# Two tokens per partition, heads in two halves, and a new opening order in a retention and MLP kernel

## The chip, the cores and the metric

The kernel runs on one core of one Trainium2 chip. The metric is the device time of one execution in microseconds; the time before is the median of three runs. A core has TensorE (PE, with its weight loads shown as PEld), VectorE (DVE), ScalarE (ACT), GpSimd (POOL) and SyncE (SP), and 16 DMA engines that serve queues of SP, ACT and POOL.

## What is computed

The first part is a retention layer over 8 batches, 8 heads, 576 tokens and a head size of 64. The second is an MLP whose hidden activation is h cos(h).

```python
scores = scale * np.matmul(q, k.transpose(0, 1, 3, 2))        # 8 x 8 x 576 x 576, scale = 1/8
gamma = 1.0 - 2.0 ** (-5.0 - np.arange(H))
Dmat = np.where(rel >= 0, gamma[:, None, None] ** rel, 0.0)   # rel = query position - key position
attn = np.matmul(scores * Dmat, v)
x = attn.transpose(0, 2, 1, 3).reshape(4608, 512)
h = x @ w_in                                                  # 512 -> 2048
out = (h * np.cos(h)) @ w_out                                 # 2048 -> 512
```

## The kernel before

**Retention.** A batch b has five chunks r: four of 128 tokens and one of 64 (`ck_of`). Since gamma^(i-j) splits into gamma^i and gamma^-j, q is multiplied by a table UQ and v by a table WV, and the causal mask MK then only cuts. For one chunk:

- `load` (L238) brings q, k and v to fp32 staging tiles `kn`, `qn`, `vn`, with one token per partition: 8 heads of 64 numbers, so runs of 256 bytes. One DMA on SP's queue for each tensor.
- `kcast` and `decay` make bf16 tiles `kq` and `vb`. For the first two batches `cast_pe` places them on named engines; later they run on POOL.
- k and q are transposed into `kqt`: for the first two batches by TensorE with an identity (`turn`, and an ACT copy out), from batch 2 on by a DMA transpose (`prep_dma`).
- `scores` (L326) multiplies k and q for each head, 64 rows of the array for each head of a pair, into the PSUM banks `sc`; DVE masks the result into `rt` (L341).
- `rest` adds up the output in PSUM bank `po`: the state of earlier chunks times q (po<-kqt,sb) plus the masked scores times v (po<-rt,vb), then the state's own update in bank `st` (st<-vb,kq), which accumulates in PSUM over the chunks of a batch. ACT copies `po` to the bf16 activations `xt` (L386) and the state to `sb` (L390).

A *visit* (b, r) is `rest(b, r-1)` followed by `scores(b, r)`.

**MLP.** Tokens go in nine blocks j of 512. `mlp1` computes one of 16 groups dt of 128 hidden units: four matmuls into a bank, the cosine on ACT (L413), the product on DVE (L416) into `gt` (block 0: `ss`). Block 0 then runs `mlp2`, 16 parts of four plain matmuls. The blocks from 1 on run `layer2`, a scheme of seven products of half size in place of eight: 14 half steps n of eight matmuls (L487), with sums of quarters made by DVE (`ssum` for activations, `tsum` once for weights; both L467), snapshots on ACT (L490) and totals on DVE (L495). The first product reads `gt` of dt 0 to 7, the second that of dt 8 to 15.

**Order.** Everything is written out by hand in `emit`; each engine runs its instructions in the order of that list, and `Sched` adds the semaphore waits. ORDER interleaves dt 0, 8, 1, 9, ... up to 7, 15. In block j, `mlp1` is followed by `layer2` with visits of batch j+1 at n = 0, 3, 6, 9 and 12 (VISITS). Batches 0 and 1 are spread by hand over the start and over block 0's `mlp2`. `idle` issues matmuls on zeros that keep TensorE active while it has no other work.

Of the kernel before, what the change touches and what calls it, by code (L numbers as in the profile page):

```python
# [12 lines left out]
DFF = 2048  # L13
# [8 lines left out]
GR = 64  # L22
NWI = 4
# [4 lines left out]
ORDER = [8 * h + i for i in range(8) for h in range(2)]  # L28
# [10 lines left out]
def ck_of(r):  # L39
    return min(CH, S_ - CH * r)  # L40

# [16 lines left out]
class Sched:  # L58
# [54 lines left out]
    def dma(self, eng, name, fn, reads=(), writes=(), after=()):  # L113
# [6 lines left out]
        d[1] += 16  # L120
        fn(self.eng[eng]).then_inc(d[0], 16)
# [12 lines left out]
class _Kernel:  # L134
    def __init__(self, nc, es, q, k, v, w_in, w_out, out):
# [10 lines left out]

        self.KQT = [sb(f"kqt{i}", [128, 2 * NP * S_], BF16) for i in range(2)]
# [3 lines left out]
        self.KQ = [[sb(f"kq{i}_{r}", [128, 2 * DM], BF16) for r in range(NCH)] for i in range(2)]  # L151
        self.bKB = [[Buf() for _ in range(NCH)] for _ in range(2)]
        self.bQB = [[Buf() for _ in range(NCH)] for _ in range(2)]
        self.VB = [[sb(f"vb{i}_{r}", [128, DM], BF16) for r in range(NCH)] for i in range(2)]
        self.bVB = [[Buf() for _ in range(NCH)] for _ in range(2)]
        self.ST32 = {x: [sb(f"{x}n{r}", [128, DM], F32) for r in range(NCH)] for x in "kqv"}
# [10 lines left out]
        self.bSB = [Buf() for _ in range(2)]  # L167
        self.GT = sb("gt", [128, 16 * TB], BF16)
# [14 lines left out]
        self.IP = sb("ip", [128, NCH], F32)  # L183
        self.WV = sb("wv", [128, NCH * H_], F32)
        self.UQ = sb("uq", [128, NCH * H_], F32)
        self.MK = sb("mk", [128, CH], BF16)
# [12 lines left out]
        self.PO, self.bPO = ps("po"), Buf()  # L199
        self.ST, self.bST = ps("st"), Buf()  # L200
# [11 lines left out]
    def consts(self):  # L212
        s = self.s
        s.op("dve", lambda e: e.memset(self.IDLE.ap(), 0.0), writes=[self.bIDLE])
        s.op("pool", lambda e: e.iota(self.IP.ap(), [[CH, NCH]], base=0, channel_multiplier=1,
                                      allow_small_or_imprecise_dtypes=True), writes=[self.bIP])
        for t, b, fill, first, cmp in ((self.ID, self.bID, 1.0, 0.0, ALU.not_equal),
                                       (self.MK, self.bMK, 0.0, 1.0, ALU.is_ge)):
            s.op("dve", lambda e: e.memset(t.ap(), first), writes=[b])
            s.op("pool", lambda e: e.affine_select(t.ap(), t.ap(), pattern=[[1, CH]],  # L220
                                                   compare_op=cmp, fill=fill, base=0,
                                                   channel_multiplier=-1), reads=[b], writes=[b])
        s.op("dve", lambda e: e.memset(self.C_LN8.ap(), float(math.log(1.0 / 8.0))), writes=[Buf()])
        s.op("dve", lambda e: e.memset(self.C_PIH.ap(), float(math.pi / 2.0)), writes=[self.bC])
        for i in range(2):
            s.op("dve", lambda e: e.memset(self.SB[i].ap(), 0.0), writes=[self.bSB[i]])
        for t, b, sign in ((self.UQ, self.bUQ, 1.0), (self.WV, self.bWV, -1.0)):
            for h in range(H_):
                s.op("act", lambda e: e.activation(  # L229
                    bass.AP(t, h, [[NCH * H_, 128], [H_, NCH]]), self.IP.ap(), AF.Exp,  # L230
                    scale=sign * self.lng[h], **(dict(bias=self.C_LN8.ap()) if sign > 0 else {})),
                    reads=[self.bIP, self.bC], writes=[Buf()])
            b.w = [Tok("act", "act", s.count["act"], {})]
        s.op("act", lambda e: e.activation(self.JUNK.ap(), self.C_PIH.ap(), AF.Sin), reads=[self.bC])  # L234
# [3 lines left out]
    def load(self, x, b, r, after=()):  # L238
        ck = ck_of(r)
        t, bt = self.ST32[x][r], self.bST32[x][r]  # L240
        dst = bass.AP(t, 0, [[DM, ck], [D_, H_], [1, D_]])
        src = bass.AP(self.src[x], (b * H_ * S_ + CH * r) * D_, [[D_, ck], [S_ * D_, H_], [1, D_]])
        return self.s.dma("sp", f"{x}n{r}", lambda e: e.dma_start(dst, src), writes=[bt], after=after)
# [16 lines left out]

    def kcast(self, eng, b, r):
        ck, i = ck_of(r), b % 2
        o, x = bass.AP(self.KQ[i][r], 0, [[2 * DM, ck], [1, DM]]), bass.AP(self.ST32["k"][r], 0, [[DM, ck], [1, DM]])
# [3 lines left out]
    def decay(self, eng, x, b, r):  # L267
        ck, i = ck_of(r), b % 2
        t, off, pitch, bt, w, bw = ((self.KQ[i][r], DM, 2 * DM, self.bQB[i][r], self.UQ, self.bUQ) if x == "q"
                                    else (self.VB[i][r], 0, DM, self.bVB[i][r], self.WV, self.bWV))  # L270
        self.s.op(eng, lambda e: e.tensor_tensor(  # L271
            bass.AP(t, off, [[pitch, ck], [D_, H_], [1, D_]]),
            bass.AP(self.ST32[x][r], 0, [[DM, ck], [D_, H_], [1, D_]]),
            bass.AP(w, r * H_, [[NCH * H_, ck], [1, H_], [0, D_]]), ALU.mult),
            reads=[self.bST32[x][r], bw], writes=[bt])

    def kqt(self, i, c, r, n=1):
        return bass.AP(self.KQT[i], c * S_ + CH * r, [[2 * NP * S_, 128], [S_, n], [1, ck_of(r)]])

    def prep_dma(self, b, r):  # L280

        s, ck, i = self.s, ck_of(r), b % 2
# [4 lines left out]
            self.kqt(i, 0, r, 2 * NP), bass.AP(self.KQ[i][r], 0, [[2 * DM, ck], [1, 2 * DM]])),  # L287
# [3 lines left out]
    def turn(self, b, r, x, eng, sc=None):  # L291

        s, ck, i = self.s, ck_of(r), b % 2
        off, c0, bs, bd = (0, 0, self.bKB[i][r], self.bKT[i][r]) if x == "k" else (DM, NP, self.bQB[i][r], self.bQT[i][r])
# [416 lines left out]
```

## Time and profile before

| | |
|---|---|
| median of 3 runs | 314.26 us (314.18 to 314.48) |
| the profiled execution | 313.65 us, of it span 311.9 us |
| mean granted TensorE clock | 0.991 |
| PE busy | 295.5 us, 95% of the span |
| DVE, ACT, POOL busy | 226.3, 179.4, 114.5 us |
| q1, the loads and DMA transposes on SP | 141,696 packets, 36.45 MB, 66.4% of the 16 DMA engines' span |
| first `mlp2` matmul | 37.85 us |
| first product of `layer2(1)` | 80.42 us |
| from there on | blocks of about 31.2 us, two of 27.4 and 16.9 us at the end |

The span runs from the first instruction to the last; the rest of the profiled execution's time lies around it. Busy time of TensorE includes the latency of each matmul, so a busy share near one does not say that the array streams all the time; for that the starts of the single matmuls are read.

### The profile page before, as it was taken

The numbers are of one execution on the slowest core, as the hardware profiler recorded it, in microseconds if no ns is written. First come the engines' busy times: TensorE is split into PE (matmuls) and PEld (weight loads), VectorE is DVE, ScalarE is ACT, GpSimd is POOL, SyncE is SP. The second block draws the span as 40 slices with busy tenths as digits, with TensorE's granted clock in tenths as the row PEclk, the third lists the DMA queues.
The fourth block names the chain that finished last, engine by engine and source line by source line (L and its number), as shares of the span: only waits on it lengthen the run. The fifth ranks groups of instructions, "written<-read, shape, count | busy, mean of one in ns | idle before, by whom it ended". The sixth has DMA issues, their size and how long they took to land.

```text
span 311.9 us, 6946 instructions
## 1 busy us (share of the span) xinstructions
PE 295.5 (95%) x2706; PEld 189.6 (61%) x2706; DVE 226.3 (73%) x372; ACT 179.4 (58%) x333; POOL 114.5 (37%) x129
## 2 busy tenths in 40 slices
PE   7679998999899999999999999999999999999994
PEld 2345445544786468646864786478647864784483
DVE  3455824789976998599659985996599659728942
ACT  7477726577455755476547654765475547427620
POOL 2364184868474655456636555430000000000000
PEclk9999997999999999999999999999999999999998
DMA  9999999999999999999999999960110011003003
GB/s 172 226 210 199 215 207 215 214 284 197 213 193 242 255 207 187 218 253 228 180 219 265 188 196 249 239 120 2 67 69 0 2 69 68 3 18 117 2 0 135
DMA packets 150560, 49.47 MB, mean 159 GB/s; under 512 B 141824, under 2 KB 145920, under 8 KB 150528
## 3 DMA queue, kind: packets, MB, share of 16 engines
q1 hardware_dynamic: 141696, 36.45, 66.4%
q0 software_dynamic: 4224, 4.19, 8.2%
q10 hardware_dynamic: 4608, 8.39, 7.7%
q8 instruction: 21, 0.34, 0.5%
q14 instruction: 11, 0.09, 0.1%
HBM read 36.70 MB, written 9.44 MB: 148 GB/s over the span
## 4 chain that ended last, share of the span: by engine, by line
PE 84%; ACT 7%; DVE 5%; issue 2%; ACTq 0%; POOL 0%; DVEq 0%; POOLq 0%
PE mm L316 59%; PE mm L318 14%; PE po L316 6%; PE sc L316 4%; DVE gt L416 3%; ACT cb L413 2%; DVE rt L341 2%; ACT kqt L302 2%; PE st L316 1%; ACT xt L386 1%; ACT sb L390 1%; ACT uq L229 1%; DVE osb L495 0%; ACT L234 0%; ACT L229 0%
## 5 line engine op out<-in xcount | busy, mean ns | idle before, releaser
L413 ACT ACTIVATE cb<-mm,c_pih 128x512 bf16<-128x512 f32 (+2 forms) x152 | 100.5, 665 | 42.5 <-PE mm L318 39.9
L316 PE MATMUL mm<-xt,win 128*128 128x512 bf16 (+2 forms) x456 | 117.3, 368 | 0.9 <-DVE gt L416 0.5
L416 DVE TENSOR_TENSOR gt<-mm,cb 128x512 bf16<-128x512 f32 x128 | 85.6, 686 | 9.1 <-ACT cb L413 7.6
L316 PEld LDWEIGHTS mm<-xt,win 128*128 128x128 bf16 x456 | 43.3, 98 | 49.8 <-ACT cb L413 1.8
L341 DVE TENSOR_TENSOR rt<-sc,mk 128x512 bf16<-128x512 f32 (+1 forms) x80 | 47.1, 629 | 32.7 <-PE sc L318 32.4
L318 PE MATMUL mm<-xt,win 128*128 128x512 bf16 (+2 forms) x152 | 55.9, 368 | 0.0
L271 POOL TENSOR_TENSOR kq<-qn,uq 128x512 bf16<-128x512 f32 (+1 forms) x39 | 42.7, 1094 | 29.1 <-DMA qn<-in_q_dram 28.1
L490 ACT ACTIVATE sn<-mm 128x512 f32<-128x512 f32 x32 | 19.1, 597 | 43.5 <-PE mm L318 43.5
L271 POOL TENSOR_TENSOR vb<-vn,wv 128x512 bf16<-128x512 f32 (+1 forms) x36 | 39.8, 1106 | 10.7 <-DMA vn<-in_v_dram 10.3
L316 PE MATMUL mm<-tt,ss 128*128 128x256 bf16 x336 | 43.3, 273 | 0.0
L264 POOL CAST kq<-kn 128x512 bf16<-128x512 f32 (+1 forms) x39 | 26.2, 671 | 46.7 <-DMA kn<-in_k_dram 40.3
L495 DVE TENSOR_TENSOR osb<-mm,sn 128x512 f32<-128x512 f32 x32 | 22.1, 689 | 29.0 <-PE mm L318 28.8
L386 ACT ACTIVATE xt<-po 128x512 bf16<-128x512 f32 (+1 forms) x41 | 22.2, 544 | 29.9 <-PE po L318 29.5
L316 PEld LDWEIGHTS mm<-tt,ss 128*128 128x128 bf16 x336 | 31.4, 98 | 4.9
L467 DVE TENSOR_TENSOR ss<-gt 128x512 bf16<-128x512 bf16 (+1 forms) x56 | 31.4, 560 | 0.9
L316 PE MATMUL mm<-wout,gt 128*128 128x256 bf16 x224 | 28.8, 273 | 2.3 <-DVE gt L416 2.2
L316 PE MATMUL mm<-wout,ss 128*128 128x256 bf16 (+1 forms) x160 | 27.9, 309 | 0.0
L318 PEld LDWEIGHTS mm<-xt,win 128*128 128x128 bf16 x152 | 14.9, 98 | 16.6
L316 PEld LDWEIGHTS mm<-wout,gt 128*128 128x128 bf16 x224 | 20.8, 98 | 6.8 <-DVE gt L416 2.3
L390 ACT ACTIVATE sb<-st 64x256 bf16<-64x256 f32 x64 | 23.8, 372 | 0.8
L316 PE MATMUL sc<-kqt 64*128 64x128 bf16 (+1 forms) x280 | 15.3, 217 | 4.1 <-ACT kqt L302 4.1
L316 PEld LDWEIGHTS mm<-wout,ss 128*128 128x128 bf16 x160 | 15.2, 98 | 5.8 <-issue 0.7
(66 smaller groups left out, 290.7 us busy)
## 6 DMA issues: line engine op xcount, KB each, us to landing
kn<-in_k_dram SPq DMA_DIRECT2D x32, 256.0 KB, 4.7
qn<-in_q_dram SPq DMA_DIRECT2D x32, 256.0 KB, 5.1
vn<-in_v_dram SPq DMA_DIRECT2D x32, 256.0 KB, 5.5
out_dram<-osb ACTq DMA_DIRECT2D x32, 256.0 KB, 3.7
win<-in_moe_w_in_dram POOLq DMA_DIRECT2D x4, 512.0 KB, 8.2
wout<-in_moe_w_out_dram POOLq DMA_DIRECT2D x4, 512.0 KB, 10.4
kn<-in_k_dram SPq DMA_DIRECT2D x8, 128.0 KB, 4.6
qn<-in_q_dram SPq DMA_DIRECT2D x8, 128.0 KB, 4.3
```

The costliest lines, as they stand in the source:

```text
L264: fn = (lambda e: e.activation(o, x, AF.Copy)) if eng == "act" else (lambda e: e.tensor_copy(o, x))
L271: self.s.op(eng, lambda e: e.tensor_tensor(bass.AP(t, off, [[pitch, ck], [D_, H_], [1, D_]]), bass.AP(self.ST32[x][r], 0, [[DM, ck], [D_, ...
L316: self.nc.tensor.matmul(o, a, b, **kw)
L318: return s.done("pe", self.nc.tensor.matmul(o, a, b, **kw), reads, writes)
L341: s.op("dve", lambda e: e.tensor_tensor(bass.AP(self.RT[r % 2][hp], 0, p3), bass.AP(self.SC[hp], 0, p3), bass.AP(self.MK, 0, [[CH, ck], [0 ...
L386: s.op("act", lambda e: e.activation(o, p, AF.Copy), reads=[self.bPO], writes=self.bXT[x0 // GR:(x0 + n) // GR])
L390: s.op("act", lambda e: e.activation(bass.AP(self.SB[r % 2], 64 * hp * 512 + 64 * hp, [[512, 64], [128, NP], [1, D_]]), bass.AP(self.ST, 6 ...
L413: s.op("act", lambda e: e.activation(ci, mi, AF.Sin, bias=self.C_PIH.ap(), scale=1.0), reads=[bm, self.bC], writes=[bcb])
L416: s.op("dve", lambda e: e.tensor_tensor(bass.AP(gt, dt * TB + o0, [[16 * TB, 128], [1, n]]), mi, ci, ALU.mult), reads=[bm, bcb], writes=bg)
L467: self.s.op(eng, lambda e: e.tensor_tensor(oo, xx, yy, op), reads=xb + yb, writes=ob)
L490: self.s.op("act", lambda e: e.activation(self.SN[k].ap(), bank[0].ap(), AF.Copy), reads=[bank[1]], writes=[self.bSN[k]])
L495: self.s.op("dve", lambda e: e.tensor_tensor(bass.AP(self.OSB, 2 * t * DM + 256 * h, [[4 * DM, 128], [DM, 2], [1, 256]]), bass.AP(bank[0], ...
```

## The change

- **Layout.** A partition now holds two neighbouring tokens of a 128-token chunk (`ns_of` = 2; 1 in the 64-token chunk) for four of the heads: partitions 0 to 63 hold heads 0 to 3, partitions 64 to 127 heads 4 to 7. A load has runs of 512 bytes (256 in the small chunk) and is issued as two DMAs, one for each half of the partitions.
- **Retention in quarters.** `scores`, the second part of `rest` and the state update use 64x64 tiles of the array: 16 matmuls for a full chunk where 8 were. The mask becomes 128 x 256 and is made from an iota.
- **State.** Output and state update share one PSUM tensor `ps` of two banks. The state is summed in an fp32 SBUF tile `s32`: an ACT copy for r = 0, a DVE add for r = 1 to 3. `state`, split from `rest`, makes the bf16 `sb` from it.
- **ORDER** ends with 6, 7, 14, 15.
- **Beginning.** The constants come in another order, ACT loads the Exp table by a `touch` at once and the Sin table after the first state; `mlp1` can put several dt of a few tokens in one bank (k, step), and pieces of block 0's `mlp1` stand between the first chunks; weight loads, casts, idles and the steps in block 0's `mlp2` are reordered; six of the `tsum` go to POOL; block 1 starts with 448 tokens of four dt; block 0's stores are issued during block 1.

```diff
+NIP = S_ // 64
-ORDER = [8 * h + i for i in range(8) for h in range(2)]
+ORDER = [8 * h + i for i in range(6) for h in range(2)] + [6, 7, 14, 15]
...
+        def half(hs):
+            dst = bass.AP(t, 64 * hs * 256 * ns, [[256 * ns, 64], [D_ * ns, 4], [1, D_ * ns]])
+            src = bass.AP(self.src[x], ((b * H_ + 4 * hs) * S_ + CH * r) * D_,
+                          [[D_ * ns, 64], [S_ * D_, 4], [1, D_ * ns]])
+            return lambda e: e.dma_start(dst, src)
+        return self.s.dma("sp", f"{x}n{r}", [half(0), half(1)], writes=[bt], after=after)
...
     def scores(self, b, r):
+        for c in range(2):
+            for sl in range(ns):
+                for hs in range(2):
+                    for hp in range(2):
+                        k0 = 64 * hp * W + 1024 * r + c * 128 + 64 * hs
+                        mms.append((
+                            bass.AP(self.SC[hp], 64 * hs * 512 + (c * ns + sl) * nq, [[512, 64], [1, nq]]),
+                            bass.AP(self.KQT[i], k0 + sl * 256, [[W, 64], [1, 64]]),
+                            bass.AP(self.KQT[i], k0 + 256 * ns, [[W, 64], [256, ns], [1, 64]]),
...
-    def rest(self, b, r):
+    def rest(self, b, r, state=True):
...
+                o = bass.AP(self.XT, x0, [[NP * XR, 128], [XR, NP], [1, ns], [ns, n // ns]])
+                p = bass.AP(self.PS, po0, [[1024, 128], [256, NP], [64, ns], [1, n // ns]])
                 s.op("act", lambda e: e.activation(o, p, AF.Copy),
+                     reads=[self.bPS], writes=self.bXT[x0 // GR:(x0 + n) // GR])
+        if state:
+            self.state(b, r)
+
+    def state(self, b, r):
         if r < NCH - 1:
+            st = bass.AP(self.PS, 128, [[1024, 128], [256, NP], [1, D_]])
+            s32 = bass.AP(self.S32, 0, [[4 * D_, 128], [D_, NP], [1, D_]])
+            if r == 0:
+                s.op("act", lambda e: e.activation(s32, st, AF.Copy), reads=[self.bPS], writes=[self.bS32])
+            else:
+                s.op("dve", lambda e: e.tensor_tensor(s32, st, s32, ALU.add),
+                     reads=[self.bS32], writes=[self.bPS, self.bS32])
             for hp in range(2):
                 s.op("act", lambda e: e.activation(
                     bass.AP(self.SB[r % 2], 64 * hp * 512 + 64 * hp, [[512, 64], [128, NP], [1, D_]]),
+                    bass.AP(self.S32, 64 * hp * 4 * D_, [[4 * D_, 64], [D_, NP], [1, D_]]), AF.Copy),
...
     def emit(self):
...
+        self.idle(12)
+        self.cast_pe(0, 0, "pool", "dve", "dve")
         self.w_in_load(0, after=[land[0][2]])
+        self.turn(0, 0, "k", "act")
+        self.idle(3)
+        self.turn(0, 0, "q", "act")
+        self.idle(6)
         self.scores(0, 0)
...
+        self.rest(0, 0, False)
+        self.idle(1)
         self.scores(0, 1)
+        self.state(0, 0)
+        self.touch(AF.Sin)
+        self.idle(6)
...
+        self.turn(0, 2, "k", "act")
+        self.decay("dve", "q", 0, 2)
+        self.rest(0, 1, False)
+        self.turn(0, 2, "q", "act")
+        self.state(0, 1)
         self.idle(2)
         self.scores(0, 2)
...
+        for dt in (0, 2):
+            self.mlp1(0, dt, 0, 256, 2)
+        self.rest(0, 2, False)
+        self.turn(0, 3, "q", "act")
+        self.state(0, 2)
         self.scores(0, 3)
+        self.mlp1(0, 0, 256, 128, 4)
...
         steps = {0: [(turn, 0, 4)], 2: [(self.scores, 0, 4)], 4: [(self.rest, 0, 4), (turn, 1, 0)],
                  6: [(self.scores, 1, 0)],
+                 7: [(turn, 1, 1), (self.rest, 1, 0, False), (self.scores, 1, 1), (self.state, 1, 0),
+                     (self.tsum, 0, 0, 4), (self.tsum, 0, 4, 4),
+                     (self.tsum, 1, 0, 4, "pool"), (self.tsum, 2, 0, 4, "pool"), (self.kcast, "pool", 1, 3),
...
+                     (self.rest, 1, 1, False), (turn, 1, 2)],
+                 8: [(self.state, 1, 1), (self.decay, "dve", "v", 1, 2)], 9: [(self.scores, 1, 2)],
+                 11: [(self.decay, "dve", "q", 1, 3), (self.rest, 1, 2, False)],
+                 12: [(turn, 1, 3), (self.state, 1, 2)], 13: [(self.decay, "dve", "v", 1, 3)],
+                 14: [(self.scores, 1, 3)]}
...
+        part1 = TB - 64
+        for n, dt in enumerate(ORDER[:4]):
+            self.mlp1(1, dt, 0, part1)
+            if n == 1:
+                self.rest(1, 3, False)
+        for dt in (0, 1):
+            self.mlp1(1, dt, part1, 64, 2, 8)
```

More of the change, by code (lines that the diff above doesn't have):

```diff
@@ L119, in dma @@
         d = self.dsem[name]
-        d[1] += 16
-        fn(self.eng[eng]).then_inc(d[0], 16)
+        for f in fn if isinstance(fn, list) else [fn]:
+            d[1] += 16
+            f(self.eng[eng]).then_inc(d[0], 16)
         clock = {s: v for s, (v, _) in self.seen[eng].items() if s != eng}
@@ L597, in emit @@
+        self.w_in_load(1, after=[land[2][1]])
+        self.turn(0, 2, "k", "act")
[3 more added lines that the diff above has]
+        self.state(0, 1)
         self.idle(2)
         self.scores(0, 2)
[L599 to L603 removed]
+        self.decay("dve", "v", 0, 2)
+        self.kcast("pool", 0, 3)
@@ L604, in emit @@
+        self.w_in_load(2, after=[land[3][1]])
         self.w_in_load(3)
+        self.decay("pool", "q", 0, 3)
+        self.w_out_load(0)
         self.turn(0, 3, "k", "act")
-        self.rest(0, 2)
+        for dt in (0, 2):
+            self.mlp1(0, dt, 0, 256, 2)
+        self.rest(0, 2, False)
         self.turn(0, 3, "q", "act")
-        self.idle(2)
+        self.state(0, 2)
         self.scores(0, 3)
-        for dt in range(4):
-            self.mlp1(0, dt, 256, 128)
+        self.mlp1(0, 0, 256, 128, 4)
@@ L612, in emit @@
+        self.decay("dve", "v", 0, 3)
+        for dt in (4, 6):
+            self.mlp1(0, dt, 0, 256, 2)
+        self.mlp1(0, 4, 256, 128, 4)
         self.rest(0, 3)
-        self.idle(4)
-        self.w_out_load(0)
+        for dt in (8, 9):
+            self.mlp1(0, dt, 0, 384)
+        self.w_out_load(1)
         self.cast_pe(0, 4, "pool", "pool", "pool")
         self.loads_to(10)
-        self.w_out_load(1)
         self.cast_pe(1, 0, "pool", "pool", "pool")
+        self.w_out_load(2)
+        self.w_out_load(3)
```

277 lines of the change are left out of this document (134 added, 143 removed).

## The prediction

> **What bounds the kernel now.** I read the page first, then busy time by stage, the waits of TensorE, and last the order of TensorE's instructions inside one retention visit.
>
> ```profile
> PE 295.5 (95%) x2706; PEld 189.6 (61%) x2706; DVE 226.3 (73%) x372; ACT 179.4 (58%) x333; POOL 114.5 (37%) x129
> PE   7679998999899999999999999999999999999994
> ```
>
> TensorE is busy 95% of the span, so time comes off only where it starts sooner, does less, or stops waiting. The slices show where it is loose: the first ten. By stage (columns: PE, PEld, DVE, ACT, POOL busy, then clock, DMA share, GB/s):
>
> ```profile
> 0.00:27.50 27.50, 20.08 (x219) 11.32 (x220) 12.24 (x30) 18.84 (x51) 13.44 (x23) 1.00 1.19 202
> 37.85:62.53 24.68, 23.27 (x234) 12.65 (x232) 12.87 (x18) 12.13 (x26) 16.98 (x19) 0.93 1.17 213
> 62.53:80.42 17.89, 16.66 (x109) 7.40 (x105) 16.82 (x26) 13.21 (x23) 11.46 (x12) 1.00 1.15 238
> 143.25:174.45 31.20, 31.09 (x312) 21.03 (x306) 24.46 (x42) 18.59 (x34) 17.40 (x19) 1.00 1.20 223
> ```
>
> A steady block (last row) has 0.1 us of idle TensorE in 31.2. The first 80.42 us, up to the first product of `layer2(1)`, is the loose part; 11 us of its busy time is `idle` matmuls, and a stretch near 50 us ran at clock 0.5. What TensorE waits for before 80.42 us (first two lines) and after it (last line):
>
> ```profile
> PE sc L316 <- ACT kqt L302: 4.1, 5, 1.2
> PE po L316 <- DVE rt L341: 1.4, 3, 0.6
> PE mm L316 <- DVE gt L416: 2.4, 5, 0.8
> ```
>
> Early it waits on the chain transpose, ACT copy, scores, DVE mask. Later it waits only where `mlp1` ends and product 0 needs the last `gt`. No DMA is in the list. Inside a visit:
>
> ```profile
> 83.13 0.41 PE L316 MATMUL po<-rt,vb 128*64 128x128 bf16 x7
> 83.38 0.29 PE L316 MATMUL st<-vb,kq 128*64 128x64 bf16 x7
> 83.60 0.39 PE L316 MATMUL sc<-kqt 64*128 64x128 bf16 x7
> 83.93 0.94 PE L316 MATMUL mm<-wout,gt 128*128 128x256 bf16 x7
> ```
>
> Eight matmuls of po take 0.25 us, st 0.22, sc 0.33. The single records explain it: the two of a pair start 3 ns apart, pairs follow at 54 ns (128 columns) or 28 ns (64). Streaming is thus 0.22, 0.12 and 0.22 us; the rest is a gap of 95 to 102 ns at each change of array shape (128x128 to 128x64, that to 64x128, that to 128x128). From po to st, both 128x64, there is none.
>
> **Retention in quarters.** A full chunk now issues 16 matmuls of 64x64 each for scores, po and st, instead of 8. If four run at once, streaming stays at 4 x 54, 4 x 54 and 4 x 28 ns. No four-way overlap is in the trace. Cost from below: none, as the pairs of 128*64 (two streams from one partition) and of 64*128 (two PSUM banks written in one partition) each already use what a quarter needs. From above: two at a time, 8 x 54 + 8 x 54 + 8 x 28, or 0.55 us more a chunk. I take none, because both kinds of pairs, and both kinds of 64*64 pairs in the half chunk, start 3 ns apart. All three groups have one shape, so the gap between st (or po) and sc goes: 0.10 us x 29 visits after 80.42 us = 2.9. The 64-token chunk has 2 quads for 4 pairs in scores and po: 2 x 0.056 x 6 batches = 0.7.
>
> **ORDER.** Product 0 reads dt 0 to 7. Dt 7 was second to last of `mlp1`, with one group (0.86 us) behind it against 0.2 + 0.70 + 0.69 us of latency, ACT and DVE. Now two groups (1.73 us) lie behind. Gaps beyond the 0.10 of the shape change, at the transitions at 112, 143, 174, 205, 236, 267 and 294 us: 0.35, 0.18, 0.09, 0.09, 0.09, 0.42, 0.88 = 2.1 us off. Product B, which needs dt 15, comes 1.75 us later: covered.
>
> **State in SBUF.** For r = 1 to 3 a DVE add (128x256 with PSUM: 0.42 us by the 128x256 row of L416) precedes the two ACT casts, and it also waits for the ACT copy out of the shared `ps`. Queued behind it on DVE are the two masks that the next `rest` needs. Mask end to next po leaves 1.23 us at most visits, but 0.10, 0.33 and 0.19 at n = 6 of the blocks at 90, 122 and 184 us, where DVE is late with `ssum`. The add starts the masks some 0.35 later: stalls of 0.3 + 0.1 + 0.25 = 0.65 us. The casts end some 0.4 us before they are needed. The strided `xt` write is not in the trace; between 0 and twice its 0.60 us, I take 0: it lies under three products. Steady sum: -2.9 - 0.7 - 2.1 + 0.65 = **-5.0 us** (-5.7 without stalls; -3 with eight of 0.35).
>
> **Loads.** Packets of q1 cost 0.664 x 16 x 311.9 / 141696 = 23 ns for 257 bytes, q10's 83 ns for 1.8 KB; so 512 bytes cost 23 to 47 ns, nearer the low end. Early landings are 1.2 us apart per 256 KB (218 GB/s), so DMA sets that pace, not SP. SP now issues six half loads a chunk; its shortest issues take 0.38 to 0.45 us, 2.3 to 2.7 us a chunk against 3.6 between chunks now. If every issue took 0.6 us the gain would be nil, without loss. Later, nothing waits on it. POOL's 64-token ops halve (1.1 to about 0.6 us), off the path.
>
> **The beginning**, walked with rows of the trace (transposes 0.22 us, ACT copy 0.60, two copies 1.09, masks 1.29, 0.25 from the last matmul to its reader):
> - The first tile lands at 3.9 us as now. Twelve idles (cold clock, 0.43 each) end at 6.3; turn k, its ACT copy to 7.3; three idles; turn q 7.2, copy to 8.2; six idles end at 8.7: scores(0,0) at 8.8 (8.48 now). No gain yet.
> - Masks to 10.5; rest(0,0) to 10.9; an idle; scores(0,1) at 11.3 (12.66), since turn(0,1) no longer waits for a rest.
> - ACT is then one chain: xt 11.1 to 11.7, s32 12.05, two sb 12.8, the Sin table (1.28 and 0.2) 14.25, copy of k(0,2) 14.85, xt(0,1) 15.4, copy of q(0,2) 15.9: scores(0,2) at 16.0 (17.66).
> - `mlp1` of dt 0 to 3 on 256 tokens (2 x 0.87) 16.6 to 18.3. DVE: masks to 17.8, v(0,2) to 18.4. rest(0,2) 18.5 to 19.15; ACT: xt to 19.95, copy of q(0,3) 20.45: scores(0,3) at 20.5 (22.77).
> - Four more `mlp1` pieces of 0.87, to 24.3, over the masks and v(0,3); rest(0,3) to 25.05; dt 8 and 9 on 384 tokens (1.3), the 128-token rests (2.2), to 28.6. Six full dt remain, 5.2, where at 27.5 now twelve do: `mlp2` starts at **33.8 against 37.85**.
> - `mlp2` stretch: 16 x 0.863 = 13.8, transposes 2.0, five scores 1.9, four rests 2.4, together 20.1. At n = 7 scores(1,1) waits for ACT and rest(1,1) for the masks just issued: 0.3 + 0.5 + 1.6 us of waits, 0.2 of it found back. End 33.8 + 22.3 = 56.1 (62.53).
> - `mlp1(1)`: 13.8; two rests, a turn, two scores 1.9; first product at **71.8 against 80.42**, -8.6.
> - Held back: the waits at n = 7 leave TensorE nearly idle for 3.4 us, as at 47 us now, where 3.4 us at half clock followed (1.7 us lost): half of that, 0.8. Six `tsum` move to POOL, 1024 elements each, by its 512-element TENSOR_TENSOR rows about 2.1 us, up to 2.9 beside DVE; POOL ends at 62 to 66 us and `prep_dma(2, 0)` queues behind them; needed at 71. With weights: 0.6. Beginning: **-7.2 us** (0 if rival 1 takes all; -9.8 if neither happens and half the waits at n = 7 are found back).
>
> Sum on the profiled execution, 313.65 us (span 311.9 and 1.8 around it): 313.65 - 7.2 - 5.0 = 301.5. The median lies 0.6 above that execution: **302.1 us**.
>
> **Rivals.**
> 1. The beginning does not pay: ACT's copies, POOL's `tsum` or w_in and w_out landing late refill what the order empties. For it: waits there are latencies of a chain, and a chain is not shortened by order. Against: the `mlp1` pieces are real work in these waits. Saving 0 to 4: 305 to 309. Chance 0.18.
> 2. Quarters overlap, but start no faster than 14 ns each on average, the densest the trace shows (st). N = 128 hides it; st costs 16 x 14 instead of 4 x 28 ns, 0.11 x 32 chunks, and the half chunks gain nothing: +4.2, 306.3. Chance 0.08.
> 3. Slower: quarters run two at a time, 0.55 us x 32 chunks + 0.11 x 8 = 18.5 us more: 320. It decides from 12.2 / 32 = 0.38 us a chunk. Against it stand the 3 ns starts. Chance 0.11.
> 4. Slower: each matmul has a start floor of its own whatever the tile. With the 28 ns between st's pairs, sixteen take 0.45 us: +0.23 + 0.23 + 0.34 a chunk, 0.34 a half chunk, x 32 and x 8: +28, 330. Against: st's eight stream in 0.12 us, where the floor would ask 0.22. Chance 0.03. [...]
>
> **Numbers.** The forecast has 0.57; rivals 1 and 2 (0.26) are faster too. Range 298.5 (steady -5.7, beginning -9.8) to 309.5 (rival 1's end): 0.83 inside. A measurement here tells 0.2% (0.6 us) from no change: faster 0.83, same 0.02, slower 0.15 (rivals 3 and 4, and 0.01 for others).
>
> **What would show it.** Quads of sc starts within 12 ns and 54 ns apart, with st to sc at no gap, or else 108 ns a quad (rival 3). The wait on DVE gt after 80 us under 0.5 us. First `mlp2` matmul near 34 us, first product of `layer2(1)` near 72; a POOL wait or clock 0.5 between is rival 1. A mask wait of some tenths at n = 6. I am wrong if blocks last over 31 us.

## The result and the profile after

The changed kernel took 312.61 us in the median, the kernel before 315.0 us in the same set of runs: ratio 0.990, 95% interval 0.9872 to 0.9929. A second set gave 0.9937 (0.9904 to 0.997). It is faster, by 2 to 3 us, not by the 12 forecast. The profiled execution of the first set ran at a mean granted TensorE clock of 0.750, with a span of 377.8 us, and one other execution of that set took 1036.24 us; no run here explains either. So the profile shown here is that of the second set: 310.0 us at 0.998, against 311.9 us at 0.991 before.

The page after, the engines' line and TensorE's slices:

```profile
PE 288.2 (93%) x3496; PEld 188.8 (61%) x3520; DVE 234.3 (76%) x392; ACT 189.9 (61%) x336; POOL 116.6 (38%) x133
PE   8579997997999998999999999998999999999994
```

TensorE is busy for 7.3 us less, but the span is only 1.9 us shorter: most of the saved work came back as idle time. By stage (the start, `mlp2` of block 0, `mlp1` of block 1 up to the first product of `layer2(1)`, one later block):

```profile
0.00:27.50 27.50, 20.06 (x288) 12.42 (x292) 14.15 (x30) 18.17 (x43) 11.44 (x22) 1.00 0.93 192
37.82:60.62 22.80, 20.52 (x286) 10.96 (x289) 13.78 (x19) 12.28 (x26) 17.05 (x16) 1.00 1.05 213
60.62:79.52 18.90, 16.48 (x155) 8.07 (x155) 14.64 (x26) 13.88 (x26) 18.90 (x18) 1.00 0.76 203
142.50:173.58 31.08, 30.51 (x399) 20.44 (x400) 26.53 (x45) 20.34 (x36) 13.36 (x15) 1.00 0.90 191
```

`mlp2` starts at 37.82 us, as before (37.85), and the first product comes at 79.52 (80.42). The later block has 0.57 us of idle TensorE where before it had 0.1. What TensorE waits for (us in total, times, longest), the three largest before 80 us and, below the dots, all after it:

```profile
PE mm L360 <- POOL kq L306: 3.4, 3, 2.6
PE sc L360 <- ACT kqt L346: 1.9, 4, 0.7
PE ps L360 <- ACT sb L454: 1.4, 1, 1.4
...
PE ps L360 <- DVE rt L387: 2.4, 4, 1.0
PE ps L360 <- ACT sb L454: 0.9, 1, 0.9
PE sc L360 <- DMA kqt<-kq: 0.6, 2, 0.3
```

The last waits on `gt` after 80 us are gone. In their place stand waits on the mask (`rt`), on `sb` and on a DMA transpose, 3.9 us together; before, none of these was there after 80 us. Ahead of 80 us, at the end of block 1's `mlp1`, 1.3 us of waits on `gt` are left. Inside a visit:

```profile
82.33 0.33 PE L360 MATMUL ps<-rt,vb 64*64 64x128 bf16 x11
82.50 0.29 PE L360 MATMUL ps<-vb,kq 64*64 64x64 bf16 x15
82.62 0.39 PE L360 MATMUL sc<-kqt 64*64 64x128 bf16 x15
82.95 0.94 PE L360 MATMUL mm<-wout,gt 128*128 128x256 bf16 x7
```

The state update takes 0.12 us from its first matmul to the first of the scores, which follow without a gap. The single records show four matmuls 3 to 4 ns apart (82.618, 82.622, 82.625, 82.628), then the next four at 82.678. The one gap left is that to the 128x128 products, 0.10 us.

### The profile page after: what moved, and what is told of

Its sections match the earlier page's. It is cut to its first block, busy times and chain, and to the rows that moved or that the text cites. A ratio compares the mean times of both kernels' runs of the same rounds, so it can differ in the third digit from the quotient of the medians.

```text
span 377.8 us, 8676 instructions
## 1 busy us (share of the span) xinstructions
PE 363.8 (96%) x3496; PEld 216.1 (57%) x3520; DVE 234.6 (62%) x392; ACT 190.1 (50%) x336; POOL 114.0 (30%) x133
## 4 chain that ended last, share of the span: by engine, by line
PE 92%; SPq 2%; DMA 2%; ACT 1%; issue 1%; DVE 0%; POOL 0%
PE mm L360 66%; PE mm L362 16%; PE ps L360 7%; PE sc L360 3%; SPq L279 2%; DMA kn<-in_k_dram 2%; ACT kqt L346 0%; DVE osb L562 0%; ACT xt L437 0%; PE sc L362 0%; ACT sb L454 0%; ACT cb L480 0%; POOL kq L306 0%; PE ps L362 0%; ACT s L449 0%
## 5 line engine op out<-in xcount | busy, mean ns | idle before, releaser
L360 PE MATMUL mm<-xt,win 128*128 128x512 bf16 (+4 forms) x500 | 144.6, 417 | 1.0 <-ACT cb L480 0.2
L480 ACT ACTIVATE cb<-mm,c_pih 128x512 bf16<-128x512 f32 (+3 forms) x147 | 99.0, 679 | 71.9 <-PE mm L362 70.7
L483 DVE TENSOR_TENSOR gt<-mm,cb 128x512 bf16<-128x512 f32 (+1 forms) x130 | 88.3, 682 | 41.3 <-ACT cb L480 39.4
L360 PEld LDWEIGHTS mm<-xt,win 128*128 128x128 bf16 x517 | 54.1, 112 | 66.4 <-issue 60.5
L362 PE MATMUL mm<-xt,win 128*128 128x512 bf16 (+5 forms) x147 | 65.6, 446 | 0.8
L387 DVE TENSOR_TENSOR rt<-sc,mk 128x512 bf16<-128x512 f32 (+1 forms) x80 | 44.8, 602 | 18.8 <-PE sc L362 18.7
L360 PE MATMUL mm<-tt,ss 128*128 128x256 bf16 x336 | 54.4, 312 | 0.0
L437 ACT ACTIVATE xt<-ps 128x512 bf16<-128x512 f32 (+1 forms) x41 | 26.9, 660 | 39.0 <-PE ps L362 28.3
L360 PE MATMUL mm<-wout,gt 128*128 128x256 bf16 x224 | 36.0, 318 | 0.0
L454 ACT ACTIVATE sb<-s 64x256 bf16<-64x256 f32 x64 | 26.5, 415 | 12.9 <-DVE s L451 11.7
L451 DVE TENSOR_TENSOR s<-ps,s 128x256 f32<-128x256 f32 x24 | 10.2, 424 | 32.5 <-ACT xt L437 32.4
L362 PEld LDWEIGHTS mm<-xt,win 128*128 128x128 bf16 x147 | 16.5, 112 | 23.1 <-issue 22.2
```

The costliest lines, as they stand in the source:

```text
L360: self.nc.tensor.matmul(o, a, b, **kw)
L362: return s.done("pe", self.nc.tensor.matmul(o, a, b, **kw), reads, writes)
L387: s.op("dve", lambda e: e.tensor_tensor(bass.AP(self.RT[r % 2][hp], 0, p3), bass.AP(self.SC[hp], 0, p3), bass.AP(self.MK, 0, [[2 * CH, 128 ...
L437: s.op("act", lambda e: e.activation(o, p, AF.Copy), reads=[self.bPS], writes=self.bXT[x0 // GR:(x0 + n) // GR])
L454: s.op("act", lambda e: e.activation(bass.AP(self.SB[r % 2], 64 * hp * 512 + 64 * hp, [[512, 64], [128, NP], [1, D_]]), bass.AP(self.S32, ...
L480: s.op("act", lambda e: e.activation(ci, mi, AF.Sin, bias=self.C_PIH.ap(), scale=1.0), reads=[bm, self.bC], writes=[bcb])
```

## The experiments

All numbers of one kernel's stages come from its one profiled execution. A stretch of TensorE at clock 0.5 begins in most of them between 12 and 54 us (before: at 50.3 us, 3.4 us long), in the kernel before also at the very end (309.7 to 311.9 us), and in four kernels (masks_first, block1_act_b, v_on_pool, both_b, with mean clocks of 0.989, 0.978, 0.972 and 0.984) also between 77 and 95 us. By the half clock alone 3.4 us of it cost up to 1.7 us. Compare times by the ratio and stages by the table, with two bounds on both. The whole change and order_only were each measured in two sets, and their ratios differ there by 0.4%. And the two executions of order_only, one kernel, differ by 2.5 us in the first stage of the table and by 1.6 us in the last, the later one with 3.4 us of half clock at 18.7 us.

| kernel | ratio to before (95%) | `mlp2` starts | first product of `layer2(1)` | from there to the end |
|---|---|---|---|---|
| before | | 37.85 | 80.42 | 231.5 |
| after_again | 0.9937 (0.9904 to 0.997) | 37.82 | 79.52 | 230.4 |
| order_only | 0.9864 (0.9821 to 0.9908) | 37.93 | 79.09 | 231.3 |
| order_only_again | 0.990 (0.9854 to 0.9947) | 40.45 | 81.22 | 229.7 |
| after_old_order | 0.997 (0.9936 to 1.0005) | 39.03 | 82.75 | 228.8 |
| new_layout_old_begin | 1.0051 (1.0015 to 1.0087) | 44.91 | 85.26 | 227.8 |
| no_pool_from_b3 | 0.9879 (0.9831 to 0.9927) | 39.31 | 82.42 | 226.6 |
| masks_first | 1.0118 (1.0071 to 1.0166) | 39.39 | 84.22 | 236.5 |
| w_in_later | 1.002 (0.999 to 1.0051) | 40.95 | 84.06 | 226.9 |
| tsum_on_dve | 0.9958 (0.9926 to 0.9991) | 38.47 | 80.68 | 228.5 |
| two_queues | 0.993 (0.990 to 0.9959) | 37.85 | 79.69 | 228.7 |
| two_queues_w | 0.9988 (0.9955 to 1.0022) | 40.44 | 83.55 | 229.8 |
| block1_act | 0.9985 (0.9952 to 1.0017) | 39.99 | 82.20 | 226.5 |
| block1_act_b | 0.9953 (0.9908 to 0.9997) | 40.30 | 81.83 | 230.7 |
| v_on_pool | 1.0185 (1.0128 to 1.0242) | 40.38 | 88.23 | 229.3 |
| both_b | 1.0156 (1.0079 to 1.0232) | 40.01 | 85.64 | 228.9 |

### The parts: ORDER, and the beginning

**after_again** is the whole change once more, beside the parts.

> The changed kernel itself, once more, for a trace at full clock. Theory S (the steady blocks save the forecast 5 us, the new beginning gives nothing or loses 1 to 2 us): first product of layer2(1) at 80 to 83 us, blocks of about 30.4 us. Theory B (the beginning saves some 7 us, the steady blocks lose what they were to save): first product at 72 to 76 us, blocks of 31.5 us or more. Both: some 3 us below the kernel before in time.

Neither theory holds alone. The first product of `layer2(1)`, at 79.52 us, is close to theory S, but the five blocks from there last 31.1 to 32.3 us where S has 30.4: the beginning gained 0.9 us and the rest 1.0.

**order_only** is the kernel before with one line changed:

```diff
-ORDER = [8 * h + i for i in range(8) for h in range(2)]
+ORDER = [8 * h + i for i in range(6) for h in range(2)] + [6, 7, 14, 15]
```

> The kernel before with the new ORDER alone (6, 7, 14, 15 last). By the forecast 2.1 us less than before: the waits on DVE gt at the ends of mlp1 after 80 us go from 2.4 us to under 0.5. If the product sums on DVE are late anyway, the wait moves to a later half step and the time stays within 0.6 us.

It gave 0.9864, twice the gain expected, and 0.990 in another set, where it stood for comparison:

> The kernel before with the new ORDER alone, once more, for comparison on the same chip: a ratio near 0.986, about 2 us under the whole change.

The whole change beside it gave 0.9937: with overlapping intervals, but the one line alone is at least as fast as all of it. **after_old_order** is the same question from the other side, the whole change with the old line put back.

> The changed kernel with the old ORDER. By the forecast 2 us slower than the changed kernel, as the waits on DVE gt return at each end of mlp1; if ORDER does nothing, within 0.6 us of it.

It gave 0.997, and its waits from 60 us on show what the old line brings:

```profile
PE mm L360 <- DVE gt L483: 4.3, 10, 0.9
```

The wait on `gt` is 4.3 us in ten places, at the end of `mlp1` of every block; with the new line 1.3 us were left, all in block 1. In the time that is only 0.3%, or 1 us, with overlapping intervals. Other waits stand against it: those on `rt` are 0.3 us in this execution and 2.4 in that of the changed kernel.

**new_layout_old_begin** keeps layout, quarters, state and ORDER of the change, and takes the emission up to block 1 from the kernel before (idles, casts, whole `rest` with its state at once, `mlp1` pieces of one dt, `tsum` on DVE, block 0's stores at once).

```diff
         self.idle(12)
-        self.cast_pe(0, 0, "pool", "dve", "dve")
...
+        self.cast_pe(0, 0, "act", "dve", "dve")
...
+        for dt in range(4):
+            self.mlp1(0, dt, 0, 256)
...
+        self.rest(0, 2)
...
-        for dt in (0, 2):
-            self.mlp1(0, dt, 0, 256, 2)
-        self.rest(0, 2, False)
```

> The changed kernel (512-byte loads, quarters, state in SBUF, new ORDER) with the emission order of before up to block 1. Theory S: as fast as the changed kernel or faster by 1 to 2 us, some 5 us below before. Theory B: near before or above it, so 3 us or more slower than the changed kernel.

1.0051, slower than before. With the old order `mlp2` starts at 44.91 us, 7 us later than before. A stretch at half clock from 14 to 24 us explains up to 5 of them by the clock alone, and perhaps more: in order_only, 3.4 us of it went with a start 2.5 us later. So the new order of the beginning does pay, by about 1.1% or 3.6 us of time. Whether it pays by shorter waits or by keeping TensorE at its clock is not separated here. It pays back what the rest of the change loses under the old order.

### The beginning: what the loads do

Two stretches of the start tell where the loss begins (DMA share and GB/s stand last; the kernel before first, the changed one second):

```profile
0.00:9.00 9.00, 6.62 (x34) 2.62 (x35) 2.51 (x10) 6.77 (x22) 2.67 (x10) 1.00 0.98 178
```

```profile
0.00:9.00 9.00, 7.36 (x45) 3.08 (x45) 3.71 (x13) 5.36 (x20) 3.13 (x11) 1.00 0.50 145
```

In the first 9 us the DMA engines were full before and are half empty now. The timeline of SP's issues at the same place, before and after, says why:

```profile
5.98 1.14 SPq L243 DMA_DIRECT2D kn<-in_k_dram  x1
7.17 1.15 SPq L243 DMA_DIRECT2D qn<-in_q_dram  x1
```

```profile
4.80 1.28 SPq L279 DMA_DIRECT2D kn<-in_k_dram  x2
6.12 1.28 SPq L279 DMA_DIRECT2D qn<-in_q_dram  x2
```

Before, SP's issues grew from 0.45 us for the first to 1.15 us for the sixth, with the DMA engines at 0.98. Now each half takes 0.617 us (the median of all half loads of the span; in the first 9 us 0.60 to 0.62 from the second on) although the DMA engines are busy for only 0.50 of the time: with the gap between them, two make 1.28 us. The packets did become cheaper for their size. Of queue q1 in the first 40 us (packets, MB, share of 16 engines), before and after:

```profile
q1 hardware_dynamic: 19345, 4.87, 70.5%
```

```profile
q1 hardware_dynamic: 10899, 4.86, 54.0%
```

That is 0.705 x 16 x 40 us / 19345 = 23 ns for packets of 252 bytes on average, and 32 ns now for 446, but in the first 9 us nothing fills the room that this leaves. Before, k of chunk 2 landed at 11.03 us; now it lands at 15.65, with w_in's first part in flight ahead of it.

**w_in_later** holds w_in back:

```diff
-        self.w_in_load(0, after=[land[0][2]])
...
         self.cast_pe(0, 1, "pool", "pool", "dve")
+        self.w_in_load(0, after=[land[2][0]])
```

> The changed kernel with the first weight load issued on POOL after the casts of chunk 1 and after k of chunk 2 has landed (about 11.5 us) instead of after v of chunk 0 (7.3 us). Theory L (v of chunk 1 and k of chunk 2 land at 14.6 and 15.7 us because w_in's 512 KB take the DMA engines, and SP with 0.62 us an issue is too slow to have them through before): they land at 11 to 12 us, turn(0, 2, k) comes 3 to 4 us earlier, the first product of layer2(1) 2 to 3 us earlier, the time falls by 1 to 3 us. Rival (the chain on ACT sets the start): scores(0, 2) stays at 18 us or more and the time within 1 us.

k of chunk 2 landed at 12.35 us, 3.3 us earlier, but k of chunk 3 at 19.78, and TensorE waited 2.9 us for its cast. Ratio 1.002: no gain.

**two_queues** takes three half loads off SP's queue:

```diff
+        if b == 0 and r == 1:
+            t0 = self.s.dma("sp", f"{x}n{r}", [half(0)], writes=[bt], after=after)
+            self.late.append((x, half(1), bt, t0))
+            return t0
...
+            t1 = self.s.dma("pool", f"{x}b", f, writes=[Buf()])
```

> The whole change, but the second halves of the loads of chunk 1 of batch 0 (k, q, v) are issued on POOL's queue at the start, so that SP issues three DMAs fewer before chunk 2. Theory (SP's issue, 0.62 to 0.66 us for each DMA, paces the early loads): k of chunk 2 lands near 13.7 us instead of 15.65, turn(0,2,k) comes near 14.5 instead of 16.4, mlp2 starts near 36 instead of 37.82, and the time falls by 1 to 2 us against the 312.7 of the whole change. Rival (the DMA engines pace them, or w_in takes them): k of chunk 2 lands within 0.5 us of before and nothing is gained.

The first links held: k of chunk 2 landed at 12.07 us (13.7 expected), and turn(0,2,k) came at 14.51 instead of 16.37. The last did not: the next chunk was then the late one. TensorE in that run, releasers in brackets:

```profile
14.51 0.33 PE L371 MATMUL mm<-ident,kq 128*128 128x128 bf16 x3
...
17.67 0.41 PE L371 MATMUL sc<-kqt 64*64 64x128 bf16 x15 [1.30 <-ACT kqt L357]
...
19.32 0.34 PE L371 MATMUL mm<-ident,kq 128*128 128x128 bf16 x3 [1.23 <-POOL kq L317]
...
23.93 0.41 PE L371 MATMUL sc<-kqt 64*64 64x128 bf16 x15 [0.69 <-ACT kqt L357]
```

scores(0,3) at 23.93 against 23.90, `mlp2` at 37.85 against 37.82, ratio 0.993 against 0.9937: nothing. **two_queues_w** holds w_in back as well:

```diff
+        self.w_in_load(0, after=[land[2][0]])
...
+        self.w_in_load(1, after=[land[3][1]])
```

> As the run with two queues, and w_in's first part is issued only when k of chunk 2 has landed, its second part when q of chunk 3 has. Theory (SP's issue and w_in together hold the early loads back): k of chunk 2 lands near 12 us and v of chunk 1 before it, mlp2 starts near 35 us, time near 310. Rival (w_in is then late for the first mlp1 pieces, or k of chunk 3 waits): a wait on w_in or on chunk 3 of 2 us or more before 25 us, and mlp2 near 37 or later.

The rival came in, with a shorter wait than it named: TensorE waited 1.6 us for w_in, `mlp2` started at 40.44 (with 3.4 us of half clock), ratio 0.9988. Three ways of moving the loads shifted the wait between chunk 2, chunk 3 and w_in, and none removed it. In the first 40 us the kernel before moves 8.06 MB at 201 GB/s and the changed one 8.07 MB at 202, with a DMA share of 1.17 from 9 us on. That the sum of bytes sets the end of the beginning fits all of this, but no run here took bytes away, so it is not shown.

### Block 1's `mlp1`

From the end of `mlp2` to the first product the stage takes 18.90 us where 15.7 were forecast. The same work takes 18.40 us in order_only (60.69 to 79.09, with 1.84 us of idles and a wait in it) and 18.68 before, so its new arrangement gained nothing in this profile. ACT's timeline in it (idle time and its releaser in brackets):

```profile
67.32 0.69 ACT L480 ACTIVATE cb<-mm,c_pih 128x512 bf16<-128x512 f32 x1 [0.17 <-PE mm L362]
69.19 0.85 ACT L454 ACTIVATE sb<-s 64x256 bf16<-64x256 f32 x2 [1.18 <-DVE s L451]
69.64 0.40 ACTq L490 DMA_DIRECT2D out_dram<-osb  x1
```

ACT stands 1.18 us for DVE's state add, because `sb` is queued ahead of the next cosines; four stores of 0.34 to 0.40 us each are issued by ACT in the same stage.

**tsum_on_dve** asks whether POOL's six `tsum` beside DVE do it, by giving them back to DVE, spread over `mlp2`:

```diff
-                     (self.tsum, 1, 0, 4, "pool"), (self.tsum, 2, 0, 4, "pool"), (self.kcast, "pool", 1, 3),
+                     (self.kcast, "pool", 1, 3), (self.cast_pe, 1, 4, "pool", "pool", "pool"),
...
+                 9: [(self.scores, 1, 2), (self.tsum, 1, 0, 4)], 10: [(self.tsum, 2, 0, 4)],
```

> The changed kernel with the six tsum of POOL spread over the mlp2 steps on DVE. Theory C (POOL's and DVE's two-operand work slow each other, so tsum and late casts on POOL cost the mlp1 of block 1 some 3 us): the bf16 sums of DVE in mlp1(1) fall from 1.2 to about 0.5 us, mlp1(1) lasts 16 to 17 instead of 18.9 us, the time falls by 1 to 3 us. Rival (DVE has no room in the mlp2 stage): that stage grows by as much.

The stage stayed long, 19.4 us (61.31 to 80.68), 0.9 of it a new wait for a DMA transpose; the ratio was 0.9958. So the six `tsum` are not what makes it long. **block1_act** splits the state into DVE's add (part 1) and ACT's casts (part 2) and moves the stores to SP's queue:

```diff
-        steps = {5: [(self.state, 1, 3)], 6: [(turn, 1, 4)], 7: [(self.store, 0, 0)], 9: [(self.scores, 1, 4)],
-                 10: [(self.store, 0, 1)], 12: [(self.store, 0, 2)], 14: [(self.store, 0, 3)]}
+        for m in range(4):
+            self.store(0, m)
+        steps = {4: [(self.state, 1, 3, 1)], 6: [(turn, 1, 4)], 8: [(self.state, 1, 3, 2)], 9: [(self.scores, 1, 4)]}
```

> The whole change, but in mlp1 of block 1 the state of chunk 3 is split (DVE's add at step 4, ACT's two casts at step 8) and block 0's four stores are issued by SP before the stage instead of by ACT inside it. Theory (ACT stands behind the state add and the store issues there): the stage from its first matmul to the first product of layer2(1) falls from 18.9 us to about 17, time lower by 1 to 2 us than 312.7. Rival (DVE, with its sums beside POOL, sets the stage): it stays within 0.4 us of 18.9.

The stage took 19.4 us again, but for another reason: one wait of 2.7 us at its end, for the DMA transpose of (2,0). SP's timeline shows what stood ahead of that:

```profile
74.49 1.25 SPq L279 DMA_DIRECT2D vn<-in_v_dram  x2
75.79 2.07 SPq L492 DMA_DIRECT2D out_dram<-osb  x4
77.90 4.51 SPq L330 DMA_TRANSPOSE kqt<-kq  x3
```

SP issues without a pause, and four stores put the transposes back by 2.07 us. Without that wait the stage would have been 16.7 us. **block1_act_b** leaves SP alone: the same split, two stores at step 15 and two at n = 2 of `layer2(1)`, on ACT.

> As block1_act (the state of chunk 3 split: DVE's add at step 4, ACT's casts at step 8 of block 1's mlp1), but the four stores stay on ACT's queue: two at the end of the stage, two at n = 2 of layer2(1). Theory (ACT behind the state add and the store issues): no wait of 2.7 us on the DMA transpose now, so the stage falls from 18.9 to 16.5 us and the time by about 2 us against the whole change, to 310 to 311. Rival (DVE beside POOL sets the stage): 18.5 or more, and no change of time.

The stage fell to 17.28 us, between theory (16.5) and rival (18.5). By these two executions, ACT's order cost 1.6 us there. The ratio, 0.9953, shows none of it: at n = 9 of `layer2(1)` (93 us) a transpose was late by 1.6 us in this run too, and 3.4 us of half clock followed at 94.39.

### The steady part: where the quarters' gain went

The waits behind the masks after 80 us come from one kind of place. DVE first, POOL below it, both from the changed kernel:

```profile
116.43 0.68 DVE L534 TENSOR_TENSOR ss<-gt,ss 128x1024 bf16<-128x1024 bf16 x1
117.03 1.55 DVE L534 TENSOR_TENSOR ss<-gt 128x1024 bf16<-128x1024 bf16 x1
118.50 1.54 DVE L534 TENSOR_TENSOR ss<-gt,ss 128x1024 bf16<-128x1024 bf16 x1
119.97 0.41 DVE L451 TENSOR_TENSOR s<-ps,s 128x256 f32<-128x256 f32 x1
120.30 1.27 DVE L387 TENSOR_TENSOR rt<-sc,mk 128x512 bf16<-128x512 f32 x2
```

```profile
116.47 1.56 POOL L315 TENSOR_TENSOR kq<-qn,uq 128x512 bf16<-128x512 f32 x1 [0.61 <-DMA qn<-in_q_dram]
117.99 1.50 POOL L315 TENSOR_TENSOR vb<-vn,wv 128x512 bf16<-128x512 f32 x1
```

The first `ssum` took 0.68 us, with an operation of POOL that began 0.04 us after it; the next two, which began while POOL was in one of its two, took 1.55 and 1.54. POOL's operations end at 118.03 and 119.49 us, and these sums 0.55 us after each, at 118.58 and 120.04. The state add comes next, then the masks, which end at 121.57 us; TensorE stood 0.89 us, to 121.67. The profile puts this wait down to `sb`, which hangs on the same add but ends at 121.26. The four waits on `rt`, at 152, 183, 211 and 216 us, have slowed sums ahead of the masks too, and all but that at 211 us the add between. POOL slowed the sums in the kernel before as well: the `ssum` after 60 us took 57.0 us of DVE then, 60.4 now, and 50.8 in no_pool_from_b3 below, where most of them have no POOL beside them. Before, the slack behind the masks of n = 6, 0.10 us at the least, just held it; the add takes 0.33.

**no_pool_from_b3** leaves out POOL's casts and decays for batches 3 to 7 (their retention then works on old tiles):

```diff
-        self.kcast("pool", b, r)
-        self.decay("pool", "q", b, r)
-        self.decay("pool", "v", b, r)
+        if b < 3:
+            self.kcast("pool", b, r)
+            self.decay("pool", "q", b, r)
+            self.decay("pool", "v", b, r)
```

> The changed kernel without POOL's casts and decays for batches 3 to 7: that part of the computation is left out, loads and transposes stay. Theory C: with POOL idle from about 95 us on, every bf16 sum on DVE takes about 0.7 us, no block after the second has a wait on DVE rt or on the state casts, and the steady part is 3 to 5 us shorter than in the changed kernel. Rival (the state add alone makes the waits): they stay, 2 us or more in all.

Its blocks from the third on are without a stall (one block by stage):

```profile
145.20:175.60 30.40, 30.40 (x402) 20.62 (x401) 24.95 (x45) 20.20 (x35) 0.00 (x0) 1.00 0.95 190
```

30.40 us with TensorE busy throughout, with the state add where it was. So the add alone costs nothing; sums that POOL slows, mostly with the add behind them, do. The ratio, 0.9879, is still no better than that of the new ORDER alone.

Where POOL's work falls makes as much of a difference. Five kernels here have the same code as the changed one from the first product of `layer2(1)` on (w_in_later, tsum_on_dve, two_queues, two_queues_w and block1_act), and from there they took 226.5 to 229.8 us, where the changed kernel took 230.4. block1_act, with 226.5, has no wait after its first product in the list, and 54.8 us of `ssum`. What shifts POOL's work into a good place, no run here shows.

**masks_first** puts the masks of a visit ahead of the state of the chunk before:

```diff
-                self.rest(b, r - 1)
+                self.rest(b, r - 1, False)
             if b < B_:
                 self.scores(b, r)
+                if r:
+                    self.state(b, r - 1)
```

> The changed kernel with one order changed in the visits of batches 2 to 7: the state add of chunk r-1 comes after the masks of scores(b, r) on DVE instead of before them. Theory M (the add, and its wait for the copy of xt on ACT, delays the masks): the waits of rest on DVE rt after 80 us, 2.4 us in the changed kernel, fall under 0.8; the time falls by 1 to 3 us. Rival (the masks are late because the bf16 sums ahead of them on DVE run at 1.5 instead of 0.7 us): the add's 0.33 us is all that is won at each late visit, under 1 us in all; or the wait moves to the state casts on ACT (sb), which now come later.

Slower, 1.0118. The waits after 80 us moved one step down the chain (in an execution of 322.55 us, 4 us over the median of this kernel):

```profile
PE ps L360 <- DVE s L451: 5.2, 3, 2.3
PE sc L360 <- DMA kqt<-kq: 3.3, 1, 3.3
PE ps L360 <- ACT sb L454: 1.7, 2, 1.4
```

`rt` is down to 0.6 us, but the state is now the late one. Of the add and the masks, the one that comes second on DVE was late in each of the two profiles.

**v_on_pool** asks why POOL runs so long: the last load is issued at 229.5 us, before it was 201.7.

```diff
-        return self.s.dma("sp", f"{x}n{r}", [half(0), half(1)], writes=[bt], after=after)
+        q = ("pool", f"{x}p{r}") if x == "v" and b > 1 else ("sp", f"{x}n{r}")
+        return self.s.dma(*q, [half(0), half(1)], writes=[bt], after=after)
```

> The whole change, but the loads of v from batch 2 on are issued on POOL's queue. Theory (SP's full queue keeps the loads from running ahead): the last load is issued near 200 us instead of 229.5, POOL is idle from there, the last two or three blocks lose their waits on DVE rt, stalls after 80 us fall from 4 to about 2 us, time lower by 1 to 3 us. Rival 1 (the buffers, not SP, pace the loads): the last load stays after 220 us and the stalls stay near 4 us. Rival 2 (POOL's own time for ten issues a block, 0.6 us each, makes more collisions with DVE): the loads do run ahead, but the stalls in the blocks before grow by 2 us or more, and the time rises.

Between theory and rival 2. The last load came at 213.2 us (206.1 in both_b), and the last three blocks with visits lost their stalls (their `layer2` 15.96 us each, against 16.88, 18.05 and 16.18). SP's queue did hold the loads back. But the time rose by 2.5% against the whole change (0.9937 in another set, to 1.0185), and the largest part of it in the profile is one instruction of DVE, here with POOL's beside it:

```profile
72.73 0.41 DVE L452 TENSOR_TENSOR s<-ps,s 128x256 f32<-128x256 f32 x1
73.06 6.55 DVE L535 TENSOR_TENSOR ss<-gt 128x512 bf16<-128x512 bf16 x1
79.53 0.68 DVE L484 TENSOR_TENSOR gt<-mm,cb 128x512 bf16<-128x512 f32 x1
```

```profile
73.56 0.63 POOL L307 CAST kq<-kn 128x512 bf16<-128x512 f32 x1
74.13 1.07 POOL L316 TENSOR_TENSOR kq<-qn,uq 128x512 bf16<-128x512 f32 x1
75.14 1.06 POOL L316 TENSOR_TENSOR vb<-vn,wv 128x512 bf16<-128x512 f32 x1
...
78.73 0.60 POOL L307 CAST kq<-kn 128x512 bf16<-128x512 f32 x1
79.30 1.22 POOL L316 TENSOR_TENSOR kq<-qn,uq 128x512 bf16<-128x512 f32 x1
```

A sum that takes 0.42 us undisturbed stood 6.55 us while POOL went through seven operations without a pause; TensorE waited 4.7 us for the `gt` behind it, and 6.8 us of half clock began in that wait. The sums at 117 and 118.5 us in the changed kernel's profile had ended 0.55 us after one operation of POOL; this one ended after seven. It also began 0.5 us before the first of them, while POOL was still issuing six loads (69.88 to 73.56); what held it then, and what let it in at last, no run shows. **both_b** joins this edit and block1_act_b.

> Both edits together. If both theories hold, 308 to 310 us, under the time of the new ORDER alone; if rival 2 of v_on_pool holds, 312 or more.

1.0156: the same event, 4.87 us long, in the same place, behind six issues of loads again.

## Why the prediction was wrong

Against the profiled execution the forecast missed by 10.3 us of span (299.7 forecast, 310.0 measured): 6.3 up to the first product of `layer2(1)` (73.2 with what was held back, 79.52 measured), 4.0 after it. The steps that failed are the price of an issue on SP, with the walk of the beginning that builds on early loads, the waits in `mlp1(1)`, put at nothing, and the stalls behind the state add, put at 0.65 us. Of the 6.3 us, 4.0 were lost up to `mlp2`, 0.5 in its stretch and 3.2 in `mlp1(1)`, less the 1.4 held back.

- **Quarters: right.** Four at a time, no gap from st to sc, and 30.40 us for a block without stalls against 31.20. Rivals 2, 3 and 4 are refuted: the sixteen of st start within 0.10 us.
- **ORDER: right in kind, too small.** 2.1 us forecast; order_only gained 1.0 and 1.4% (3.1 and 4.3 us). The sum left out the first transition, at 79 to 80 us (0.8 us), and block 1's stage. In the changed kernel the line takes away 3.0 of 4.3 us of waits on `gt`, but its time differs by only 1 us.
- **State in SBUF: the term that failed in the steady part.** 0.65 us of stalls forecast, 3.9 measured, so that the steady part gained 1.0 us and not 5.0. The kind of place was found, but its cost was read off one execution in which `ssum` happened to be slowed at three visits. Where POOL's work falls decides, and that moved: its loads now last to 230 us. In the execution of block1_act, with the same state add, the steady part took 226.5 us, just what was forecast; that a forecast of this kind holds in one execution and not in another is luck as long as nothing fixes POOL's place.
- **Loads: the step that failed first.** Between 0.38 to 0.45 us for an issue and the 0.6 that the text gave as its other end, the lower was taken; measured, 0.617. And "without loss" at 0.6 was wrong: SP becomes the pace of the first 9 us (DMA share 0.50), and has little room later (20.6 us of waits from 80 to 230 us, before 47.7 from 80 to 200). "Later, nothing waits on it" fails with it: the last load is issued at 229.5 us and not at 201.7, and four stores added to SP in block1_act showed up as a late transpose. How much of the time this step cost is not shown: two_queues brought k of chunk 2 forward by 3.6 us, and `mlp2` not at all. The trace shows the price on SP: two issues of 0.617 us for one tensor.
- **The beginning.** scores(0,0) and (0,1) came at 8.20 and 12.00 (8.8 and 11.3 forecast); the walk breaks at turn(0,2,k), at 16.37 with POOL's cast of a late k ahead of it, so scores(0,2) came at 18.87 instead of 16.0. From there it loses about another 1 us: scores(0,3) 3.4 us late, `mlp2` 4.0 late at 37.82. The `mlp2` stretch was right (22.80 against 22.3). "Cold clock, 0.43 each" in the walk is, in the trace of before, twelve idles that follow each other at 0.43 us, against 0.21 at 7.4 us, both at a granted clock of 1.00. The 0.8 us held back for the clock rest on one place of that trace, where TensorE was busy for 2.00 of the 3.40 us from 47 us on and then ran at 0.51 for 3.4 us; that the one brings the other, no run shows, and in the changed kernel the `mlp2` stretch ran at 1.00.
- **`mlp1(1)`:** 15.7 forecast, 18.90 measured. The sum counted TensorE's work and put waits at nothing; 2.4 us of waits are in the profile. ACT stands behind the state add and issues four stores. 1.6 us of the 3.2 went in block1_act_b's execution; the rest is open.
- **Rival 1 was the case** in its effect (the beginning saved 0.9 us), and half in its cause: not ACT's copies or `tsum`, but loads and w_in. A second loss, in the steady part, it did not name. The range stopped at 309.5 because no case had both.

No version here beats the kernel before with the new ORDER alone by more than its interval.

## What to carry to other kernels

When a load is split into two DMAs, price the issuing queue by what an issue takes with room in the DMA engines (0.617 us here), and ask what else that queue carries for the whole run. A gain of TensorE in a block was kept here where the other engines had slack at the visit where they are latest (30.40 us in no_pool_from_b3, 31.08 with the slowed sums): cost an added DVE operation there (0.33 us for this add, with 0.10 of slack), with DVE's sums at their slowed duration (1.55 us, not 0.68). When a change has several parts, measure the smallest one alone: here one line of order gave at least as much as the whole change.

## What was not expected of the hardware

- An issue of a half load on SP's queue took 0.617 us even with the DMA engines half empty (share 0.50 in the first 9 us); packets of 446 bytes on average cost 32 ns, those of 252 bytes 23.
- A bf16 sum on DVE that began during an operation of POOL took 1.55 us instead of 0.68 (changed kernel, 117 us), and another, in v_on_pool, 6.55 us, through seven operations of POOL, where it takes 0.42 us undisturbed.
